# Another hand-written order for units 1 to 6 of phase one of a pooled-attention and snake-activation kernel

## The chip, the cores and the metric

The program runs on one NeuronCore of one Trainium2 chip. The metric is device microseconds of that core for one execution. Before the change three runs took 917.28, 917.67 and 918.19 us; the median, 917.67 us, is the time before.

## The reference

Attention of 8 batches with 8 heads, 576 rows and 64 columns, whose keys and values are means over 8 rows (72 pooled rows are left); its output, 4608 tokens by 512, goes through a layer of 2048 with the activation h + sin(alpha h)^2 / alpha:

```python
k_p = k.reshape(B, H, Sp, pool, D).mean(axis=3)
v_p = v.reshape(B, H, Sp, pool, D).mean(axis=3)
scores = scale * np.matmul(q, k_p.transpose(0, 1, 3, 2))
scores = scores - np.max(scores, axis=-1, keepdims=True)
attn = np.exp(scores)
attn = attn / (np.sum(attn, axis=-1, keepdims=True) + 1e-09)
x = np.matmul(attn, v_p)          # then to (4608, 512)
h = x @ w_in
s = np.sin(alpha * h)
out = (h + s * s / (alpha + 1e-09)) @ w_out
```

All arrays are float32.

## The kernel before, in words

**Two phases.** Phase one computes the attention and g = h + sin^2 / alpha and stores g to a buffer in HBM (`g_bridge`); phase two (from about 520 us) loads g and multiplies by w_out. Both large products are written with seven block products in place of eight (names M1 to M7); in phase one the products 1 and 5 of most groups are split once more in the same way ("inner products", steps i.a to i.e).

**Units and groups.** Phase one runs over 9 units of 512 columns of x (u = 0 to 8), each of 4 groups J = 0 to 3. A group multiplies a quarter of w_in: `M2`, `M6`, `M3`, `M7`, `M4` (line 930), each in four pieces (`M2.0` to `M2.3`), and M5 as well in group 1. Inner products (line 1020) of group J of units 2 to 6, and of groups 1 to 3 of unit 1, have the steps a, b, d, e1 and e5 on TensorE, with copies ca, cm, cb on ScalarE (lines 1033, 1037, 1040) and one sum ad on VectorE (line 1043) between them: b waits for ca, d for cb, e1 and e5 for ad. ScalarE copies partial sums from one PSUM bank to another (c16, c67, p5; line 911) and computes sines and squares (s00, s01, s10, s11, q00, q01, q1; lines 998 and 1005); VectorE adds them up (a00, a01, a11, f10, f1; line 910). f1 alone of these adds two SBUF operands (128 x 1024); the others read one operand from PSUM. `st` stores a group's g, 1 MB in two DMAs (line 1053); its tile is one of two, so a00 of the group after next waits for the store.

**The attention beside it.** While unit u (1 to 6) runs, the attention of batch u + 1 is done in its gaps: scores0 and scores1 (line 405), the shifts by the maximum (shift0 to shift3 name four calls that take the next of a list, so a swap of two names alone changes nothing; lines 425, 426), the exponentials (line 451), the sums and scalings norm0 to norm3 (VectorE lines 457, 458, GpSimd line 459), 32 x 32 transposes turn0 to turn3 on VectorE (lines 591 to 601) into the tile `tr`, sixteen DMAs `move` from `tr` to another partition quarter each (line 611), the products with v (`values`, lines 700, 713) and the copies out0 to out4 of the result (line 627). Beside it the operands of the batches behind are made ready: `load_q` (lines 185, 206) for unit u + 2, its transposes qa, qb, qc into `tr` (lines 318, 321) and sixteen DMAs back from `tr`, eight in qd and eight in qe (line 331); load_k0 and load_k1 (line 222) and load_v (lines 241, 246), and their sums over 8 rows on GpSimd: pool_k0, pool_k1, pool_vm (line 232, the large tile of v) and pool_v (lines 232, 252, the small rest). scores0 reads what qd wrote, scores1 what qe wrote too. k_t and k_c turn the pooled keys (lines 363, 367). load_k0, load_k1 and load_v take turns on two buffers named `kvin`; load_k1 waits until the first of the two that is pooled, in program order, is read.

**What sets the order.** Nothing is scheduled by the compiler: each engine and each DMA queue works through its instructions in program order, and that order comes from a list of actions with a number each. The tables `ORDER` (lines 42 to 138) give the numbers: "U" for the attention's actions in units 1 to 6, "mid0" to "mid3" for the four groups of units 1 to 6 (two groups are exceptions: the first of unit 1 uses "enter", the last of unit 6 "exit", neither of which changes). An action of table "U" stands at 28 u plus its number, one of a group at 7 (4 u + J) plus its number; `perform` sorts and emits them:

```python
for m, f in acts.items():
    if m in where:
        self.at(7 * n + where[m], f)
...
self.agenda.sort(key=lambda x: x[:2])
while self.agenda and self.agenda[0][0] < until:
    self.agenda.pop(0)[2]()
```

Waits between engines follow from the data, whatever the numbers. All DMAs of phase one's units 1 to 6 are issued by SyncE (SP), one queue; a DMA also waits until the one issued eight before it has landed.

Of the kernel before, what the change touches and what calls it, by code (L numbers as in the profile page):

```python
# [67 lines left out]
    "a00": 2.6351, "a11": 2.7835, "M3.1": 3.71335, "M3.2": 3.97525, "M3.3": 5.35825, "M4.0": 5.57345, "a01": 5.76695, "M4.1": 6.46705, "M4.2": 9.07915,  # L68
    "M4.3": 9.1098, "s11": 9.29485, "s10": 9.36555, "q1": 9.36695, "s01": 9.43775, "q01": 9.4416, "f1": 9.6118, "f10": 9.61195, "st": 10.05},
"end3": {  # L70
    "M5.0": -5.29345, "M5.1": -4.88305, "M1.0": -2.98805, "M1.1": -2.4027, "M1.2": -2.23625, "M5.2": -1.2153, "M1.3": -1.07205, "c16": 2.27975,
    "M6.0": 2.32495, "M6.1": 2.33055, "M6.2": 2.3529, "M2.0": 2.3654, "M6.3": 2.3726, "c67": 2.37425, "M2.1": 2.38685, "M2.2": 2.4012, "M5.3": 2.40185,
    "M7.0": 2.41595, "M2.3": 2.4234, "M7.1": 2.4277, "M7.2": 2.46025, "p5": 2.48725, "M3.0": 2.53015, "M7.3": 2.5939, "a11": 2.612, "M3.1": 2.6266,
    "s00": 2.7151, "q00": 2.82195, "s11": 2.9428, "M3.2": 2.96575, "M3.3": 2.96605, "a01": 3.3439, "M4.0": 3.50965, "a00": 3.60325, "M4.1": 3.9026,
    "M4.2": 4.2433, "M4.3": 4.37135, "s01": 4.63625, "q01": 4.6412, "s10": 4.64555, "q1": 6.5869, "f1": 6.6127, "f10": 6.6139, "st": 10.05},
"enter": {
    "M1.0": -0.48095, "M1.1": -0.4801, "M1.2": -0.4681, "M5.0": -0.45225, "M5.1": -0.44225, "M1.3": -0.4418, "M5.2": 0.0977, "M5.3": 0.1635, "c16": 0.2794,
    "p5": 0.86945, "M6.0": 2.04465, "M2.0": 3.2741, "M6.1": 6.62085, "M6.2": 6.6329, "M6.3": 6.6653, "M2.1": 6.6889, "M2.2": 6.8691, "M2.3": 7.1328,
    "c67": 7.13695, "s00": 7.13705, "q00": 7.13865, "a00": 9.0381, "M7.0": 10.78275, "M7.1": 10.8224, "M3.0": 10.85505, "M3.1": 10.97425, "M7.2": 11.40445,
    "M3.2": 11.41515, "M3.3": 11.59405, "M7.3": 11.633, "a01": 11.64185, "a11": 11.7721, "s01": 11.88975, "M4.0": 11.9007, "M4.1": 11.96155,  # L80
    "M4.2": 12.03945, "M4.3": 12.084, "q01": 12.2488, "s11": 12.2491, "s10": 12.51005, "q1": 13.17745, "f10": 13.40255, "f1": 13.6228, "st": 15.95645},
# [1493 lines left out]
```

## Time and profile before

| what | value |
|---|---|
| three runs, us | 917.28, 917.67, 918.19 |
| span of the profiled execution, first to last instruction, us | 915.5 |
| mean granted TensorE clock | 1.000 |
| TensorE busy, whole span | 98% |
| VectorE, ScalarE, GpSimd busy, whole span | 74%, 50%, 23% |
| units 2 to 5: start of the first scores, us | 147.7, 204.8, 262.1, 318.6 |
| start of the first scores of unit 6, us | 376.4 |
| mean busy share of the 16 DMA engines, 92 to 440 us | 0.63 |

The spans of one execution are shorter than its time by what lies around them; the profile does not say which of the three times belongs to the profiled execution. In the profile a matmul in float32 is two rows (two passes); rows of the timeline merge equal instructions that follow each other, with the start, the length, and in brackets the idle time of the engine before it and what ended it. In a row of waits the numbers are the total in us, how often, and the longest. In a row of windows they are the length and the busy us (with the number of instructions) of PE, its weight loads, VectorE (DVE), ScalarE (ACT) and GpSimd (POOL), then the granted clock, the DMA share and GB/s.

### The profile page before, as it was taken

The page shows a single profiled execution, that of the slowest core. Times are in us where ns is not written, and L with a number is a line of the kernel's source. Part 1 is how long each engine was busy: PE and PEld are TensorE (multiplying, and loading weights), DVE is VectorE, ACT ScalarE, POOL GpSimd, SP SyncE. Part 2 cuts the span into 40 slices and gives each one's busy share as a digit, 9 for nine tenths or more (in the row PEclk, how much of TensorE's full clock was granted, in tenths as well). Part 3 has the DMA queues.
Part 4 walks back from the last instruction along what each step waited for, and adds up shares of the span by engine and source line. Part 5 has one row for each costly group of instructions (what it writes and reads, how often), then busy time and mean ns, then how long its engine had stood idle before and what let it go on. Part 6 is the DMA issues. An engine that isn't in the chain of part 4 may idle for free.

```text
span 915.5 us, 18344 instructions
## 1 busy us (share of the span) xinstructions
PE 896.1 (98%) x7146; PEld 815.8 (89%) x7146; DVE 679.6 (74%) x1016; ACT 455.4 (50%) x1073; POOL 210.8 (23%) x235
## 2 busy tenths in 40 slices
PE   8999999999999999999999999999999999999998
PEld 5787888878788887888888899999999999999997
DVE  7576856768667585674466989978888888989895
ACT  5686877868778686787785722112111112112111
POOL 4689651733517334150000000000000000000000
PEclk9999999999999999999999999999999999999999
DMA  9946766666756766545627237171617253433501
GB/s 260 241 151 180 211 193 165 193 201 174 206 153 191 206 170 188 144 133 161 239 93 247 92 108 224 37 224 27 221 39 189 72 170 91 155 105 112 148 15 40
DMA packets 128751, 141.17 MB, mean 154 GB/s; under 512 B 46920, under 2 KB 95704, under 8 KB 128664
## 3 DMA queue, kind: packets, MB, share of 16 engines
q1 hardware_dynamic: 125880, 137.88, 51.6%
q10 hardware_dynamic: 2784, 2.11, 0.9%
q8 instruction: 57, 0.93, 0.4%
q14 instruction: 30, 0.25, 0.1%
HBM read 75.37 MB, written 47.19 MB: 134 GB/s over the span
## 4 chain that ended last, share of the span: by engine, by line
PE 79%; SPq 5%; DVE 4%; DMA 4%; ACT 3%; POOL 2%; issue 2%; ACTq 0%; DVEq 0%; POOLq 0%
PE PS L1306 42%; PE PS L930 28%; SPq L331 3%; DVE h L910 3%; PE PS L1020 3%; DMA kvin<-in_k_dram 2%; PE PS L700 2%; SPq L611 2%; DMA q<-tr 1%; POOL kvin L232 1%; PE PS L405 1%; ACT s L998 1%; ACT s L1005 1%; PE PS L713 1%; DMA ex<-tr 1%
## 5 line engine op out<-in xcount | busy, mean ns | idle before, releaser
L930 PE MATMUL PS<-home,a 128*128 128x256 f32 x968 | 250.1, 382 | 0.0
L930 PEld LDWEIGHTS PS<-home,a 128*128 128x128 f32 x968 | 177.9, 190 | 29.2 <-issue 5.0
L930 PE MATMUL PS<-home,as 128*128 128x256 f32 x728 | 194.6, 382 | 0.1
L930 PEld LDWEIGHTS PS<-home,as 128*128 128x128 f32 x728 | 132.7, 190 | 17.5 <-ACT PS L911 1.7
L1306 PE MATMUL PS<-s,wb 128*128 128x144 f32 x896 | 119.2, 286 | 0.4 <-ACT PS L1434 0.4
L1306 PEld LDWEIGHTS PS<-s,wb 128*128 128x128 f32 x896 | 113.6, 190 | 0.6 <-ACT PS L1434 0.6
L1356 POOL TENSOR_TENSOR cc<-cc,cb 128x576 f32<-128x576 f32 x1 | 2.0, 1981 | 484.6 <-DVE cb L1261 484.6
L1005 ACT ACTIVATE s<-s,c 128x256 f32<-128x256 f32 (+1 forms) x216 | 112.5, 580 | 0.0
L910 DVE TENSOR_TENSOR h<-PS,s 128x512 f32<-128x512 f32 x72 | 48.2, 683 | 74.8 <-ACT s L1005 72.9
L1434 ACT COPY PS<-PS 128x144 f32<-128x144 f32 x56 | 14.7, 263 | 144.4 <-PE PS L1306 144.3
L232 POOL TENSOR_TENSOR kvin<-kvin 96x768 f32<-96x768 f32 (+3 forms) x42 | 71.6, 1705 | 23.9 <-DMA kvin<-in_k_dram 15.8
L1306 PE MATMUL PS<-r,wb 128*128 128x144 f32 x512 | 73.2, 286 | 0.0
L1306 PE MATMUL PS<-s,a 128*128 128x144 f32 x512 | 73.2, 286 | 0.0
L910 DVE TENSOR_TENSOR h<-h,s 128x1024 f32<-128x1024 f32 x36 | 49.2, 1366 | 30.4 <-ACT s L1005 30.3
L998 ACT ACTIVATE s<-h,al 128x256 f32<-128x256 f32 x144 | 63.5, 502 | 13.1 <-DVE h L910 13.0
L1306 PEld LDWEIGHTS PS<-r,wb 128*128 128x128 f32 x512 | 67.1, 190 | 0.1
L1306 PEld LDWEIGHTS PS<-s,a 128*128 128x128 f32 x512 | 67.0, 190 | 0.0
L998 ACT ACTIVATE s<-PS,al 128x256 f32<-128x256 f32 x144 | 60.5, 475 | 11.2 <-PE PS L930 8.8
L910 DVE TENSOR_TENSOR h<-PS,p 128x512 f32<-128x512 f32 x72 | 49.0, 685 | 18.5 <-PE PS L930 9.8
L911 ACT COPY PS<-PS 128x512 f32<-128x512 f32 x72 | 41.6, 578 | 40.3 <-PE PS L930 16.8
L459 POOL TENSOR_TENSOR ex<-ex,sm 128x576 f32<-128x576 f32 (+1 forms) x28 | 36.0, 1300 | 108.9 <-DVE sm L458 108.2
L1454 ACT COPY PS<-PS 128x144 f32<-128x144 f32 x56 | 14.7, 263 | 89.4 <-PE PS L1306 89.4
(217 smaller groups left out, 1536.1 us busy)
## 6 DMA issues: line engine op xcount, KB each, us to landing
g_bridge<-h SPq DMA_DIRECT2D x72, 512.0 KB
r<-g_bridge SPq DMA_DIRECT2D x31, 1152.0 KB
out_dram<-o SPq DMA_DIRECT2D x122, 72.0 KB
kvin<-in_k_dram SPq DMA_DIRECT2D x14, 576.0 KB
q<-in_q_dram SPq DMA_DIRECT2D x7, 1024.0 KB
kvin<-in_v_dram SPq DMA_DIRECT2D x14, 512.0 KB
ex<-tr SPq DMA_DIRECT2D x54, 92.0 KB
ex<-tr SPq DMA_DIRECT2D x54, 88.0 KB
```

What stands on the lines that cost most here:

```text
L232: self.nc.gpsimd.tensor_tensor(out=t[..., 0:w] if w > D else out, in0=t[..., 0:w], in1=t[..., w:2 * w], op=OP.add)
L331: nc.sync.dma_start(out=qm[32 * c:32 * c + 32, to:to + w], in_=tr[32 * a:32 * a + 32, k, at:at + w])
L459: nc.gpsimd.tensor_tensor(out=E(i), in0=E(i), in1=sm.unsqueeze(2).to_broadcast([P, n, Sp]), op=OP.mult)
L611: queue.dma_start(out=self.aT[r:r + 32, a, 0:w], in_=tr[32 * a:32 * a + 32, c, s, 0:w])
L700: nc.tensor.matmul(o[r:r + 64], w, x, start=start and i < 2, stop=False, skip_group_check=True)
L910: add = lambda o, x, y: nc.vector.tensor_tensor(out=o, in0=x, in1=y, op=OP.add)
L911: copy = lambda o, x: nc.scalar.copy(out=o, in_=x)
L930: nc.tensor.matmul(ps[:, jj, :], self.A[p][:, kk, f * P:(f + 1) * P], x[:, kk, :], start=(start and part == 0), stop=(kk == 1), skip_group ...
L998: self.nc.scalar.activation(out=G.s[:, i, jj, j, :], in_=src[:, jj], func=AF.Sin, scale=self.al[:, f:f + 1])
L1005: self.nc.scalar.activation(out=x, in_=x, func=AF.Square, scale=self.c[:, f:f + 1])
L1020: nc.tensor.matmul(out, W[m][:, G.J], self.X2[p][m], start=start, stop=True, skip_group_check=True)
L1306: nc.tensor.matmul(out, W[:, J // 2, J % 2, :], A[:, J, :], start=(start and J == 0), stop=(J == self.NJ - 1), skip_group_check=True)
```

## The change

Only numbers of the tables "U", "mid0", "mid1", "mid2" and "mid3" change; the other tables are wrapped differently and hold what they held. No instruction is added or removed. In the tables below each line is from the file; the lines of the other tables, that differ in their wrapping alone, are left out.

```diff
 "U": {
-    "load_k0": -3.31225, "load_v": -0.96965, "scores0": 3.279, "shift0": 5.5894, "shift1": 5.6395, "scores1": 7.66855, "shift2": 7.69635, "exp1": 10.5847,
-    "exp0": 11.4077, "exp2": 11.40805, "shift3": 11.6083, "exp3": 11.73155, "norm0": 11.785, "norm1": 11.8859, "norm3": 11.919, "norm2": 11.9294,
-    "pool_vm": 11.9323, "pool_v": 11.9332, "pool_k0": 12.01065, "turn1": 12.15105, "turn3": 12.264, "turn2": 12.2775, "load_q": 13.4176, "turn0": 15.964,
-    "load_k1": 17.85695, "move": 24.04575, "clean": 24.12855, "values": 24.12865, "qa": 24.1287, "out4": 24.12875, "pool_k1": 24.12885, "out0": 24.12885,
-    "qc": 24.12885, "qb": 24.12895, "mark": 24.12895, "out2": 24.129, "sx0": 24.1291, "inner_x": 24.12915, "out3": 24.33175, "k_t": 24.4364, "k_c": 24.4956,
-    "qd": 24.7856, "out1": 24.87145, "sx1": 24.87995, "sx2": 25.5786, "qe": 26.19775, "sx3": 33.60825},
+    "load_k0": -3.31225, "load_v": -0.96965, "scores0": 3.279, "shift1": 5.61994, "shift0": 7.14828, "scores1": 7.66855, "shift2": 7.69635,
+    "exp1": 11.39419, "exp0": 11.40678, "shift3": 11.6083, "exp2": 11.69571, "exp3": 11.73155, "norm0": 11.85811, "norm2": 11.9294, "norm1": 11.93006,
+    "norm3": 11.93036, "pool_k0": 11.93266, "pool_v": 11.93269, "pool_vm": 11.9327, "turn2": 12.31331, "turn3": 12.32741, "turn1": 12.34345,
+    "load_q": 13.4176, "load_k1": 13.54022, "turn0": 15.964, "move": 24.04575, "clean": 24.12855, "values": 24.12865, "qc": 24.12868, "qa": 24.1287,
+    "out4": 24.12875, "pool_k1": 24.12885, "out0": 24.12885, "qb": 24.12895, "mark": 24.12895, "out2": 24.129, "sx0": 24.1291, "inner_x": 24.12915,
+    "out3": 24.33175, "k_t": 24.4364, "k_c": 24.4956, "qd": 24.64897, "out1": 24.87145, "sx1": 24.87995, "qe": 24.96216, "sx2": 25.5786,
+    "sx3": 33.62096},
...
 "mid0": {
-    "i.a": -3.44775, "i.ca": -3.11535, "i.cm": -3.1115, "i.b": -3.11065, "i.cb": -3.1106, "i.d": -2.748, "i.ad": -1.9601, "i.e5": -0.69805, "p5": 2.55425,
-    "i.e1": 2.87235, "c16": 3.3461, "M2.0": 3.50525, "M2.1": 4.52555, "M6.0": 5.9571, "M2.2": 5.9617, "M2.3": 5.96715, "M6.1": 6.2838, "M6.2": 7.6624,
-    "M6.3": 7.66535, "s00": 7.835, "q00": 8.92395, "c67": 9.6177, "a00": 10.37115, "M3.0": 11.33615, "M3.1": 11.33625, "M7.0": 11.34, "M3.2": 11.34015,
-    "M7.1": 11.4021, "M3.3": 11.41255, "a01": 11.6089, "M7.2": 11.68785, "M7.3": 11.70765, "s01": 11.7474, "a11": 11.8728, "M4.0": 11.9812, "M4.1": 12.0337,
-    "M4.2": 12.03755, "M4.3": 12.0423, "s11": 12.2488, "s10": 12.24975, "q1": 12.4368, "q01": 12.8354, "f10": 12.95975, "f1": 12.96, "st": 13.86795},
+    "i.a": -3.44775, "i.ca": -3.11535, "i.cm": -3.1115, "i.b": -3.11065, "i.cb": -3.1106, "i.d": -2.748, "i.ad": -1.9601, "i.e5": -0.69805,
+    "p5": 2.55425, "i.e1": 2.87235, "c16": 2.92563, "M2.3": 4.30308, "M6.1": 5.96453, "M2.2": 5.96455, "M2.0": 5.96456, "M6.2": 6.04054,
+    "M2.1": 6.30017, "M6.0": 6.77211, "M6.3": 7.50001, "s00": 7.835, "c67": 8.14526, "M3.2": 8.48782, "q00": 8.92395, "M7.0": 9.2981, "a00": 10.37115,
+    "M3.0": 11.33615, "M7.1": 11.4021, "M3.1": 11.40333, "M3.3": 11.41255, "a01": 11.6089, "M7.3": 11.68745, "M7.2": 11.68785, "s01": 11.7474,
+    "a11": 11.86757, "s11": 11.89308, "M4.2": 11.92875, "M4.1": 11.94559, "M4.0": 11.9812, "M4.3": 12.0423, "s10": 12.24975, "q01": 12.2689,
+    "q1": 12.30265, "f1": 12.96, "f10": 13.64418, "st": 13.86795},
 "mid1": {
-    "i.a": 4.34025, "i.ca": 4.3997, "M5.0": 4.40225, "i.b": 4.4051, "i.cb": 4.4067, "i.cm": 4.4072, "M5.1": 4.415, "i.d": 4.41525, "i.ad": 4.61795,
-    "M5.2": 4.68665, "i.e1": 4.6893, "c16": 4.6958, "M6.0": 4.70895, "M2.0": 4.71385, "M6.1": 4.71905, "M6.2": 4.85125, "M6.3": 4.88645, "M2.1": 4.9164,
-    "M2.2": 4.9175, "M2.3": 4.9216, "M5.3": 4.9236, "c67": 4.9407, "s00": 4.9412, "M3.0": 5.0296, "M7.0": 5.0386, "M7.1": 5.0393, "M3.1": 5.10295,
-    "q00": 5.1499, "a00": 5.2457, "p5": 5.24655, "M7.2": 5.26125, "M7.3": 5.26325, "a11": 5.3567, "M3.2": 5.4866, "M3.3": 5.9075, "M4.0": 5.9184,
-    "a01": 5.95985, "M4.1": 5.9935, "M4.2": 6.1266, "M4.3": 7.29135, "s10": 7.7045, "s01": 7.82565, "s11": 7.82645, "q1": 7.8273, "f10": 9.63095,
-    "q01": 10.3848, "f1": 10.57355, "st": 17.5694},
+    "i.a": 4.34025, "i.ca": 4.3997, "i.b": 4.4051, "i.cm": 4.40677, "i.cb": 4.40681, "M5.0": 4.41522, "i.d": 4.41525, "i.ad": 4.61795,
+    "M5.2": 4.68665, "i.e1": 4.6893, "c16": 4.6958, "M6.0": 4.70895, "M2.0": 4.71385, "M6.1": 4.71905, "M6.2": 4.85125, "M6.3": 4.90912,
+    "M2.1": 4.9164, "M2.2": 4.9175, "M2.3": 4.9216, "M5.1": 4.92644, "M5.3": 4.93039, "c67": 4.9407, "s00": 4.9412, "M3.0": 5.00874, "M7.0": 5.04209,
+    "M7.1": 5.04209, "M3.1": 5.10295, "q00": 5.1499, "p5": 5.21406, "a00": 5.2457, "M7.3": 5.25744, "M7.2": 5.26125, "a11": 5.3567, "M3.3": 5.9075,
+    "M3.2": 5.9142, "M4.0": 5.9184, "a01": 5.95985, "M4.2": 5.96632, "M4.3": 5.96725, "M4.1": 5.9935, "s01": 7.82565, "s10": 7.91743, "s11": 7.9648,
+    "q1": 8.02211, "f10": 9.63095, "q01": 10.3848, "f1": 10.57355, "st": 17.5694},
 "mid2": {
-    "i.a": -2.3038, "i.cm": -1.7518, "i.ca": -1.7514, "i.b": -1.7503, "i.cb": -1.7501, "i.d": -1.735, "i.ad": -1.59855, "i.e1": -1.0348, "c16": -0.57955,
-    "M6.0": 0.29225, "M2.0": 0.293, "i.e5": 0.29845, "M6.1": 0.33965, "M6.2": 0.3757, "M6.3": 0.39735, "M2.1": 0.41675, "M2.2": 0.4244, "M2.3": 0.5874,
-    "c67": 1.0048, "s00": 1.0277, "q00": 1.0698, "p5": 1.70115, "a00": 1.96485, "M7.0": 2.16015, "M7.1": 2.53405, "M3.0": 2.6511, "M7.2": 2.70895,
-    "M7.3": 2.7296, "M3.1": 2.8176, "M3.2": 2.9094, "M3.3": 3.08845, "a11": 3.2776, "a01": 3.78395, "s11": 3.99815, "M4.0": 4.0048, "s01": 4.0872,
-    "M4.1": 4.23675, "M4.2": 4.25385, "M4.3": 4.44025, "s10": 9.67355, "q1": 9.71865, "f10": 10.1286, "q01": 10.88815, "f1": 11.0343, "st": 11.5035},
+    "i.a": -2.3038, "i.cm": -1.7748, "i.ca": -1.7514, "i.b": -1.7503, "i.cb": -1.7501, "i.d": -1.735, "i.ad": -1.59855, "i.e1": -1.0348,
+    "c16": -0.57955, "M6.1": -0.42395, "M6.0": -0.01556, "M6.3": 0.37336, "M2.1": 0.37512, "M6.2": 0.3757, "M2.0": 0.39898, "M2.2": 0.47325,
+    "M2.3": 0.59072, "i.e5": 0.69826, "c67": 1.0048, "s00": 1.0277, "q00": 1.21555, "a00": 1.96485, "M3.2": 2.08265, "p5": 2.22096, "M7.0": 2.57527,
+    "M3.0": 2.6511, "M7.2": 2.70895, "M7.3": 2.7296, "M7.1": 2.7919, "M3.1": 2.8176, "M3.3": 3.08845, "a11": 3.2776, "M4.0": 3.73108, "a01": 3.78395,
+    "s11": 3.99815, "s01": 4.0872, "M4.1": 4.10256, "M4.2": 4.26342, "M4.3": 4.44025, "s10": 9.71301, "q1": 9.71865, "f10": 10.1286, "q01": 10.88815,
+    "f1": 11.0343, "st": 11.5035},
 "mid3": {
-    "i.a": -6.2122, "i.cm": -5.4897, "i.ca": -4.6089, "i.b": -4.1596, "i.cb": -3.09295, "i.d": -3.08935, "i.ad": -3.08745, "i.e1": -2.73575, "c16": 1.9205,
-    "i.e5": 2.24095, "p5": 2.8146, "M6.0": 2.95315, "M6.1": 2.99055, "M2.0": 3.0069, "M6.2": 3.03045, "M6.3": 3.0506, "M2.1": 3.07885, "c67": 3.10355,
-    "M2.2": 3.17395, "M7.0": 3.2504, "M2.3": 3.37095, "M3.0": 3.3757, "M3.1": 3.552, "M7.1": 3.5522, "s00": 3.61515, "M7.2": 3.6319, "M7.3": 3.6631,
-    "q00": 3.85525, "a00": 3.8687, "a11": 3.8995, "M3.2": 4.0691, "M4.0": 4.2482, "M3.3": 4.2522, "a01": 5.04005, "M4.1": 5.62885, "M4.2": 6.2931,
-    "M4.3": 9.7245, "s10": 10.13465, "s11": 13.67425, "q1": 13.86355, "s01": 14.5847, "q01": 18.3923, "f1": 18.6301, "f10": 18.85055, "st": 19.1827},
+    "i.a": -5.44769, "i.cm": -5.07042, "i.ca": -4.6089, "i.b": -4.1596, "i.cb": -3.09295, "i.d": -3.08935, "i.ad": -3.08745, "i.e1": -2.73575,
+    "c16": 1.9205, "i.e5": 2.24095, "p5": 2.8146, "M6.2": 3.03045, "M6.0": 3.03297, "M2.0": 3.03902, "M6.3": 3.0506, "M6.1": 3.06611, "M2.1": 3.07812,
+    "c67": 3.12872, "M2.3": 3.19906, "M2.2": 3.37148, "M7.1": 3.37179, "M3.2": 3.40969, "M7.0": 3.55213, "M3.1": 3.55217, "M7.3": 3.60051,
+    "s00": 3.61515, "M7.2": 3.6319, "M3.0": 3.77507, "q00": 3.85525, "a00": 3.8687, "a11": 3.8995, "M4.0": 3.95088, "M3.3": 3.96749, "a01": 5.04005,
+    "M4.2": 5.27798, "M4.1": 6.29603, "s11": 10.02061, "M4.3": 10.06132, "s10": 10.13465, "s01": 11.30312, "q1": 13.86355, "q01": 18.61556,
+    "f1": 18.6301, "f10": 18.80556, "st": 19.1827},
```

What that makes of the order on the engines in a unit (from the two built programs, unit 3):

- SP before: load_k0 of the next unit, qd, store of group 2, qe, load_v; after: qd, load_k0, qe, store of group 2, load_v. And before: store of group 0, load_k1, the moves; after: load_k1, store of group 0, the moves.
- GpSimd before: norm0, norm1, norm3, norm2, pool_vm, pool_v, pool_k0; after: norm0, norm2, norm1, norm3, pool_k0, pool_v, pool_vm. Then, as before, clean (a memset) and pool_k1.
- VectorE: norm and turn in other orders (turns 2, 3, 1 for 1, 3, 2; a00 of group 1 ahead of them); f10 of group 0 behind f1 and ahead of turn0; a11 of group 0 ahead of the second norm; f10 of the unit before ahead of norm0; qc ahead of qa.
- ScalarE: c16 of group 0 ahead of the sines s10, s11 of the unit before; s11 of group 0 ahead of c67 of group 1; the order of q01 and q1, of s01 and s10 of groups 0 and 1, of c67 and the square beside it, and of two exponentials and the copies cb and cm beside them; the small copy within `values` (line 707) ahead of c67 of group 3.
- TensorE: products of one group or of two neighbours exchanged. Between i.d and i.e1 of group 3 stand M4.1 and M4.2 where M4.0, M4.1 and M4.2 stood; in group 1, M5.1 stands behind M2.3 and no longer ahead of i.d; i.e5 of group 2 stands behind M2.3 where it stood behind M2.0.

55 rows, old and new, of the table ORDER are left out of this document.

## The prediction

> **What bounds the kernel now.** I read the busy shares first, then the busy time unit by unit in phase one (a unit is four groups on 512 columns; its scores start at 147.7, 204.8, 262.1, 318.6 and 376.4 us), then what TensorE (PE) waited for there, then the timeline around each wait.
>
> ```profile
> PE 896.1 (98%) x7146; PEld 815.8 (89%) x7146; DVE 679.6 (74%) x1016; ACT 455.4 (50%) x1073; POOL 210.8 (23%) x235
> 204.80:262.10 57.30, 55.30 (x471) 47.05 (x470) 39.57 (x64) 42.91 (x97) 24.32 (x28) 1.00 0.65 185
> 318.60:376.40 57.80, 55.19 (x470) 47.53 (x469) 37.96 (x64) 42.76 (x97) 23.69 (x28) 1.00 0.60 172
> PE PS L405 <- DMA q<-tr: 4.0, 5, 1.1
> PE PS L700 <- DMA ex<-tr: 3.8, 3, 1.8
> PE PS L1020 <- DVE PS L1043: 1.9, 2, 1.0
> ```
>
> PE is busy 98%, at a granted clock of 1.00. A unit needs 55.1 to 55.3 us of PE and takes 56.5 to 57.8: order can win only the difference. From 92 to 440 us three waits make up nearly all of it: 4.0 us in the second scores (q's last piece, units 2 to 6: 1.12, 0.87, 0.63, 0.79, 0.56), 3.8 in the values (softmax moves, units 1, 4, 5: 1.26, 0.72, 1.81), 1.9 in the inner products of group 3 (units 2, 3). Sum 9.7; nothing the change touches can give more.
>
> ```profile
> 201.81 0.89 SPq L1053 DMA_DIRECT2D g_bridge<-h  x2
> 202.75 7.03 SPq L331 DMA_DIRECT2D q<-tr  x8
> 211.36 1.00 PE L405 MATMUL PS<-kblk,q 64*64 64x72 f32 x46 [0.87 <-DMA q<-tr]
> 346.34 0.90 SPq L1053 DMA_DIRECT2D g_bridge<-h  x2
> 347.33 0.82 SPq L222 DMA_DIRECT2D kvin<-in_k_dram  x1
> 348.25 12.88 SPq L611 DMA_DIRECT2D ex<-tr  x16
> 362.79 0.65 PE L700 MATMUL PS<-ex,vm 64*64 64x512 f32 x6 [1.81 <-DMA ex<-tr]
> 225.79 3.73 POOL L232 TENSOR_TENSOR kvin<-kvin 128x1024 f32<-128x1024 f32 x2
> 231.37 1.26 DVE L910 TENSOR_TENSOR h<-h,s 128x1024 f32<-128x1024 f32 x1
> 240.47 3.74 POOL L232 TENSOR_TENSOR kvin<-kvin 96x768 f32<-96x768 f32 x2 [2.95 <-DMA kvin<-in_k_dram]
> 240.53 2.83 DVE L910 TENSOR_TENSOR h<-h,s 128x1024 f32<-128x1024 f32 x1
> ```
>
> The reader sees three late things. The last eight q copies (qe) stand behind the store of group 2, which waits for its last addition until 201.8, so they end at 209.8 and land at 211.2. The sixteen moves stand behind the second k load: its 576 KB go first, and issue stops for it. And f1 takes 2.83 us where its median is 1.23, because a k addition on GpSimd (POOL) began 0.06 us before it.
>
> **q copies first (qd, qe).** The sixteen q copies now stand ahead of the next unit's first k load (qd) and of group 2's store (qe). In unit 3 qd ended at 256.3; then the k load (0.82) and eight copies of about 0.64 (move rows: 11.37 for sixteen, less a 0.8 pause) end near 262.4 and land 1.5 later, 264; the second half of the scores wants them near 267.5. Cover 3.5 us: the whole 4.0 us goes. Late next is the store: issued near 262.5 instead of 259.1, it lands 4.5 later, 267, and its buffer is wanted by the next unit's a00 at 269.4: 2.4 us of cover, cost nothing; uncovered it would delay a00, then a01 and the inner sum, at most by what is missing. The k load, 9 us later, is first read after the next softmax (282 in unit 4). The v load behind the store starts earlier than before.
>
> **k pooled and loaded ahead of the moves.** POOL now does k's sums (3.56) first, then the small v sums (2.5), then the large ones (4.5). The second k load needs a free buffer; that comes from k's sums at about 229.4 in unit 3, not from the large v sums at 230.3, and its place is now ahead of group 0's store (232.66), which it leaves alone. The moves then stand right behind that store and the last turn (233.44) instead of starting at 234.57 with a pause of 0.8 (in unit 5, 1.5 to 2.7 lost). They end some 1.9 us earlier, 3 in unit 5. Units 1, 4, 5 lacked 1.26, 0.72 and 1.81, but PE also arrives earlier by the q wait (0.6 to 0.9): just enough in unit 5. I take 3.2 of 3.8; in unit 1 the margin below is thin. Bounds 1.5 and 3.8. The large v sums end near 237; their reader starts at 248.8.
>
> **f1 of group 1 and the inner sum behind it.** With k landed near 234, the second k pooling follows at about 237 and ends near 241, so f1 (240.5, or a little before) meets its tail, not its head: some 0.3 lost, not 1.6. But the order also takes a product pair away between inner step d and step e1 of group 3 (two of 0.432 us, there were three). DVE's chain behind ACT's copy ca is 0.9 (q01) + 1.22 (f1) + 0.6 + 0.7 = 3.4, plus hand-over 0.1; PE's way from ca is 0.1 + 0.88 + 0.86 + 0.45 + 0.86 = 3.15. So a wait of up to 0.35, less where PE reaches step b late: 0.2 in each of six units, 1.2 new (bounds 0 and 2.1), against 1.9 removed.
>
> **Products, copies and turns exchanged.** Work is neither added nor removed. I followed unit 3 product by product. c16 of group 0 moves ahead of the sine s10; a00 of group 1 ahead of the turns (224.9 to about 224.4), which lets ca of group 2 keep up with its inner products, now 0.43 earlier; f10 of group 0 goes behind f1, so f1 is 0.69 earlier and the turn where it was. M5.1 moves out of the stretch before c16 of group 1, leaving that copy about 0.05 of cover where it had 0.56. In group 2 ACT runs from c16's end (232.41) to ca's end (239.68) in 7.27 while PE needs 7.87 to step b: 0.6 of cover. Five such places have under 0.15 left; I price them at 0.15 a unit, 0.9 (bounds 0 and 3.0, half a microsecond a unit).
>
> **Sum.** 4.0 + 3.2 + 1.9 - 1.2 - 0.9 = 7.0 less. The profiled span is 915.5; the runs are 917.28 to 918.19, so some 2.2 lie around it. 915.5 - 7.0 + 2.2 = 910.7. Its own range: best 4.0 + 3.8 + 1.9 = 9.7, giving 908.0; worst 4.0 + 1.5 + 1.9 - 2.1 - 3.0 = 2.3, giving 915.4.
>
> **Rivals.** A, slower: f1 of group 0 is caught by the large v sums. Their first step takes 2.37 us, and now starts behind k's and the small v sums, 0.05 + 3.56 + 2.5 = 6.1 after the last softmax product on POOL. f1 started 5.54 after it in units 2 to 5 (225.83 to 231.37) and 6.45 in unit 1; without f10 ahead it is 4.85 and 5.76. So 1.25 and 0.34 of margin; the rival decides as soon as f1 comes later than 6.1. Behind f1 wait the turn, the store and the next group's sines; of 2.37 ACT's cover takes 0.3, so 2.1 in each of units 1 to 5, 10.5 in all: 910.7 + 10.5 = 921.2. For it: 2.83 above; at 125.96 an f1 that began 0.02 before a k step took 1.22. Against it: the margin, and that PE, from which f1 follows, comes earlier. The Trainium skill, "SBUF — State Buffer", section "Who interferes with whom", states it as a lock: a vector operation with two SBUF inputs and a GpSimd operation that reads SBUF exclude each other, and whichever is issued first holds the ports to its end. By that rule the additions with one PSUM input are safe; the trace agrees (92 of them between 92 and 440 us, none over 0.69 us).
>
> B: the moves stay late, because the store's 1 MB now stands directly ahead of them as k did, and the exchanged products cost their bound: 4.0 + 1.0 - 2.1 = 2.9, giving 914.8. For it: moves share the queue with the store in every unit. Against: in unit 3 the store had landed at 237.1, before the moves were eight deep.
>
> C: nothing is gained, since ACT's chain takes over from the copies that land: if f1 and the sines behind it hold ca back by 1.2 us in each of six units, 7.2 more, 917.9. For it: the small covers. Against: ACT is busy 43 of 57 us in a unit and waits for PE more than PE for it.
>
> **How the numbers follow.** Forecast 0.67, A 0.12, B 0.12, C 0.09. A measurement of this kernel can tell 0.2%, 1.8 us, from no change: faster means under 915.8. Faster 0.67 + 0.12 = 0.79, same 0.09, slower 0.12. The range starts at 907.5, just under the best case, and ends at 917.0, so A and most of C lie outside.
>
> **What would show it.** After: no wait of the second scores (L405) for q copies; the values (L700) wait for moves in no unit, or in unit 1 alone; the k load (L222) issued before the store of group 0; f1 (L910, h from h and s) under 1.6 us everywhere; a short new wait of L1020 for the inner sum (L1043). Wrong it would be if f1 of group 0 shows 2 us and more, if waits of L930 or L1020 for ACT add up to over 3 us, or if a00 waits for a store.

## The result and the profile after

Four runs of the changed kernel took 907.51, 907.82, 909.42 and 911.21 us, median 908.62. Four runs of the kernel before on the same chip took 917.28 to 918.33, median 917.93. The ratio is 0.9898, with a 95% interval of 0.988 to 0.9915: about 1% faster. The forecast was 910.7, its range 907.5 to 917.0. The profiled execution took 907.51 us and spans 905.7 us (before: 915.5).

All line numbers of the changed kernel are higher by 9: L405 is now L414, L700 is L709, L910 is L919, L911 is L920, L930 is L939, L1020 is L1029, L1033 is L1042, L1043 is L1052.

First the busy shares of the changed kernel:

```profile
PE 896.0 (99%) x7146; PEld 815.0 (90%) x7146; DVE 677.4 (75%) x1016; ACT 456.6 (50%) x1073; POOL 206.3 (23%) x235
```

TensorE (PE) is busy for the same 896 us as before, in a shorter span: the gain is idle time of PE. All that the rows show of PE's waits between 92 and 440 us (total, times, longest):

```profile
PE PS L1029 <- ACT PS L1042: 0.9, 1, 0.9
PE PS L939 <- ACT PS L920: 0.6, 1, 0.6
```

All three rows of before that the prediction names (4.0 for q, 3.8 for the moves, 1.9 for the inner sum) are gone, and so is a fourth (0.4 for ScalarE, in unit 1). In their place stand 1.5 us of waits for ScalarE, both in unit 1. The busy time unit by unit, changed kernel, units 1 to 4 (length, then busy us of PE, weight loads, DVE, ACT, POOL):

```profile
91.22:147.71 56.49, 54.88 (x466) 46.63 (x465) 40.14 (x64) 41.37 (x93) 28.53 (x38) 1.00 0.67 191
147.71:202.66 54.95, 54.95 (x470) 47.00 (x469) 37.99 (x64) 43.02 (x97) 23.52 (x28) 1.00 0.67 192
202.66:257.40 54.74, 54.74 (x471) 46.88 (x470) 38.02 (x64) 43.03 (x97) 23.53 (x28) 1.00 0.69 194
257.40:312.09 54.69, 54.69 (x470) 46.98 (x470) 38.02 (x64) 43.03 (x97) 23.54 (x28) 1.00 0.67 192
```

From unit 2 on the length of a unit is the recorded busy time of PE, to the hundredth; unit 1 alone keeps 1.6 us of idle time. Busy time is not yet a floor, though. In these traces a product of 128x256 is recorded with 0.38 us, while the next one starts 0.22 after it when nothing holds it up, so a hold-up of up to 0.16 us hides in the product ahead of it, and a longer one hides as much. That is why a unit's busy time is smaller than the 55.1 to 55.3 of before: it held a part of the waits that are gone. The scores of unit 3, for instance, were busy for 3.07 us before and for 2.78 after, with the q wait gone.

The q copies, the store and the second half of the scores in unit 3; then the k load, the store, the moves and the values in unit 5 (SyncE's queue and PE, changed kernel):

```profile
196.63 5.52 SPq L340 DMA_DIRECT2D q<-tr  x8
202.25 1.07 SPq L1062 DMA_DIRECT2D g_bridge<-h  x2
207.48 1.53 PE L414 MATMUL PS<-kblk,q 64*64 64x72 f32 x80
...
334.87 0.33 SPq L231 DMA_DIRECT2D kvin<-in_k_dram  x1
338.26 0.98 SPq L1062 DMA_DIRECT2D g_bridge<-h  x2
339.67 11.51 SPq L620 DMA_DIRECT2D ex<-tr  x16
353.47 0.65 PE L709 MATMUL PS<-ex,vm 64*64 64x512 f32 x6
```

The copies end at 202.15, 0.5 us before unit 3's first scores; before they ended 4.9 us after them. The scores at 207.48 wait for no copy. The moves of unit 5 start 27.6 us after the unit's first scores (29.6 before), end at 351.2, which is 3.4 us earlier in the unit (the forecast said 3), and the values at 353.47 come without a wait.

For the rest I use one sum per profile, worked out from the start times of matmul rows: the **stretch**, from unit 1's first scores to phase two's first product. It leaves out the start, where loads arrive: unit 1's first scores came between 90.6 and 94.3 us in the profiles of this study. It took 433.45 us before and 423.70 after, 9.75 less; the span fell by 9.8.

### The profile page after: what moved, and what is told of

Read it like the earlier page. It is cut to its first block, busy times and chain, and to the rows that moved or that the text cites. A ratio compares the mean times of both kernels' runs of the same rounds, so it can differ in the third digit from the quotient of the medians.

```text
span 905.7 us, 18360 instructions
## 1 busy us (share of the span) xinstructions
PE 896.0 (99%) x7146; PEld 815.0 (90%) x7146; DVE 677.4 (75%) x1016; ACT 456.6 (50%) x1073; POOL 206.3 (23%) x235
## 4 chain that ended last, share of the span: by engine, by line
PE 95%; ACT 2%; DVE 2%; issue 0%; DMA 0%; ACTq 0%; DVEq 0%
PE PS L1315 42%; PE PS L939 39%; PE PS L1029 7%; PE PS L414 2%; PE PS L709 2%; DVE h L919 1%; PE PS L722 1%; ACT s L1007 1%; ACT s L1014 1%; PE PS L1087 0%; PE PS L523 0%; PE PS L502 0%; PE PS L372 0%; PE PS L485 0%; DMA out_dram<-o 0%
## 5 line engine op out<-in xcount | busy, mean ns | idle before, releaser
L939 PE MATMUL PS<-home,a 128*128 128x256 f32 x968 | 252.2, 382 | 0.0
L939 PEld LDWEIGHTS PS<-home,a 128*128 128x128 f32 x968 | 177.5, 190 | 28.9 <-issue 5.0
L939 PE MATMUL PS<-home,as 128*128 128x256 f32 x728 | 196.8, 381 | 0.6 <-ACT PS L920 0.6
L939 PEld LDWEIGHTS PS<-home,as 128*128 128x128 f32 x728 | 133.9, 190 | 17.7 <-ACT PS L920 1.0
L919 DVE TENSOR_TENSOR h<-PS,s 128x512 f32<-128x512 f32 x72 | 48.5, 686 | 81.7 <-ACT s L1014 81.7
L919 DVE TENSOR_TENSOR h<-h,s 128x1024 f32<-128x1024 f32 x36 | 48.2, 1340 | 29.8 <-ACT s L1014 29.8
L920 ACT COPY PS<-PS 128x512 f32<-128x512 f32 x72 | 41.4, 575 | 40.4 <-PE PS L939 16.1
L1315 PE MATMUL PS<-s,we 128*128 128x144 f32 x384 | 55.0, 286 | 0.7 <-ACT PS L1418 0.7
```

What stands on the lines that cost most here:

```text
L919: add = lambda o, x, y: nc.vector.tensor_tensor(out=o, in0=x, in1=y, op=OP.add)
L920: copy = lambda o, x: nc.scalar.copy(out=o, in_=x)
L939: nc.tensor.matmul(ps[:, jj, :], self.A[p][:, kk, f * P:(f + 1) * P], x[:, kk, :], start=(start and part == 0), stop=(kk == 1), skip_group ...
L1315: nc.tensor.matmul(out, W[:, J // 2, J % 2, :], A[:, J, :], start=(start and J == 0), stop=(J == self.NJ - 1), skip_group_check=True)
```

## The experiments

Each kernel was timed beside the kernel before on the same chip, and the chips differ, so ratios are compared, not microseconds alone. The stretch and the units are those of one profiled execution each.

| kernel | median us (runs) | ratio to before, 95% | stretch, us | units 1 to 5, us |
|---|---|---|---|---|
| before | 917.93 (4) | 1 | 433.45 | 56.06, 57.16, 57.26, 56.51, 57.82 |
| after | 908.62 (4) | 0.9898 (0.988 to 0.9915) | 423.70 | 56.49, 54.95, 54.74, 54.69, 54.88 |
| q_only | 912.92 (5) | 0.9912 (0.9892 to 0.9931) | 428.37 | 56.32, 55.68, 55.92, 56.29, 56.38 |
| k_only | 914.95 (5) | 0.9932 (0.9912 to 0.9951) | 431.23 | 56.82, 58.48, 55.67, 56.20, 55.43 |
| qk | 908.37 (4) | 0.9864 (0.9842 to 0.9886) | 423.47 | 56.44, 54.63, 54.80, 55.04, 54.78 |
| mid_only | 917.82 (11) | 0.9969 (0.9954 to 0.9985) | 435.41 | 55.41, 60.15, 56.11, 57.73, 57.10 |
| q_back | 913.16 (8) | 0.9946 (0.9926 to 0.9966) | 428.04 | 56.54, 57.01, 55.53, 55.53, 55.48 |
| guard | 905.75 (4) | 0.9866 (0.9849 to 0.9883) | 421.99 | 54.29, 55.02, 54.87, 54.83, 55.02 |
| vm_first | 905.35 (4) | 0.9858 (0.9843 to 0.9872) | 421.92 | 54.71, 54.89, 54.73, 54.70, 54.89 |
| qk_vm | 906.47 (4) | 0.9866 (0.983 to 0.9902) | 423.11 | 56.00, 54.71, 54.81, 54.67, 55.14 |
| collide | 906.96 (4) | 0.9866 (0.9839 to 0.9892) | 422.40 | 54.61, 54.89, 54.74, 54.70, 54.88 |
| after_third | 908.29 (4) | 0.9878 (0.985 to 0.9906) | 423.84 | 56.69, 54.88, 54.74, 54.70, 54.88 |
| caught | 911.79 (5) | 0.9919 (0.9893 to 0.9944) | 427.67 | 55.86, 55.99, 55.76, 55.73, 56.38 |

### The parts alone: q_only, k_only, qk, mid_only

Four numbers of the table "U" for k, two for q (the entries stand apart in the table); `qk` has both, all on the kernel before. `mid_only` has the new group tables with the old table "U".

```diff
 # q_only
-    "qd": 24.7856, "qe": 26.19775,
+    "qd": 24.64897, "qe": 24.96216,
 # k_only
-    "pool_vm": 11.9323, "pool_v": 11.9332, "pool_k0": 12.01065, "load_k1": 17.85695,
+    "pool_k0": 11.93266, "pool_v": 11.93269, "pool_vm": 11.9327, "load_k1": 13.54022,
```

> The kernel before with qd and qe alone moved (qd ahead of the next unit's first k load, qe ahead of the store of group 2). Theory (three separate late things, each worth its own wait): no wait of the second scores for q copies, 4.0 us less in that row; but PE then reaches the values up to 0.9 us earlier per unit with the moves where they were, so 1 to 2 us come back as waits of the values (L700) for moves: 914.5 to 916. Rival (the waits add up independently): 4.0 less in all, 913.9. Rival (ACT's chain takes over): no change, 917.9.

> The kernel before with pool_k0, pool_v, pool_vm in this order and load_k1 ahead of the store of group 0, nothing else. Theory: the values wait for moves in no unit (3.8 us less), f1 of group 1 is 1.3 us in units 2 and 3 (1.9 less of waits L1020 for L1043); q's wait of 4.0 stays. But f10 still stands ahead of f1 of group 0, so f1 starts 5.5 us after the last softmax product on POOL in units 2 to 5 and 6.4 in unit 1, against 6.1 for the first large v sum: unit 1 collides (f1 over 3 us), units 2 to 5 just miss. 912.5 to 914.5. Rival A (the collision in all units): f1 of group 0 over 3 us in five units and the time at 918 or more.

> Both of these together in the kernel before, all products, copies, turns and softmax steps as they were. Theory: the two parts carry the whole gain and the exchanges none: 908 to 910.5, as the changed kernel, and waits for q copies and for moves both gone. Rival (the exchanges are needed, because the chains of ACT and VectorE bind once PE is not held by DMA): 912 or more, with waits of L930 and L1020 for ACT and DVE that the changed kernel does not have.

> The four tables of the groups from the changed kernel with the attention's table of the kernel before. Theory: the order of products alone removes no DMA wait; q's 4.0 and the moves' 3.8 stay, the inner sum's 1.9 stays: 916.5 to 919. Rival (the exchanges of products are what gains): 913 or less.

What PE waited for from 92 to 440 us, q_only:

```profile
PE PS L700 <- DMA ex<-tr: 5.0, 4, 1.5
PE PS L1020 <- DVE PS L1043: 0.9, 1, 0.9
PE PS L1020 <- ACT PS L1033: 0.5, 1, 0.5
```

the same of k_only:

```profile
PE PS L405 <- DMA q<-tr: 4.3, 5, 2.0
PE PS L700 <- DMA ex<-tr: 0.9, 1, 0.9
PE PS L930 <- ACT PS L911: 0.6, 1, 0.6
PE PS L1020 <- ACT PS L1033: 0.3, 1, 0.3
```

of qk:

```profile
PE PS L700 <- ACT PS L911: 0.5, 1, 0.5
PE PS L930 <- ACT PS L911: 0.5, 1, 0.5
PE PS L1020 <- ACT PS L1033: 0.5, 1, 0.5
```

and of mid_only (its lines are 8 higher than those of before):

```profile
PE PS L708 <- DMA ex<-tr: 4.6, 5, 1.8
PE PS L413 <- DMA q<-tr: 4.3, 5, 2.0
PE PS L1028 <- DVE PS L1051: 0.3, 1, 0.3
```

Each part takes away its own wait (all of q's, 2.9 of 3.8 for the moves), and what is left of the other grows: without the q wait PE comes earlier at the values and waits 5.0 us for the moves where it waited 3.8; with the moves earlier it waits 4.3 for q where it waited 4.0, with a longest of 2.0 in place of 1.1. The stretch falls by 5.1 us with q alone, 2.2 with k alone, 10.0 with both.

That looks as if the two parts together were worth 2.7 us more than the two added, but two of these profiles hold something else. The granted clock was 0.50 for 3.4 us of unit 2 in k_only (first row) and in mid_only (second row):

```profile
154.99:158.40 3.41, 3.25 (x50) 2.87 (x51) 1.90 (x3) 1.18 (x3) 0.00 (x0) 0.50 0.90 190
156.26:159.66 3.40, 3.40 (x12) 2.87 (x11) 1.61 (x2) 0.54 (x2) 0.00 (x0) 0.50 1.02 202
```

Four products of 128x256 took 1.89 us there (k_only, at 156.81), where they take 1.03 otherwise. No other profile of the table has such a piece. Half of 3.4 is 1.7 us, an estimate of what it cost at most; it is in the 58.48 and 60.15 us of unit 2. So k alone is worth between 2.2 and 3.9, and the two together 1.0 to 2.7 more than the parts added. The times show no such thing: 0.88% less for q alone and 0.68% for k alone make 1.56%, and both together took 1.36% less (1.14 to 1.58). Whether the parts help each other stays open; that each makes the other's wait longer is shown.

`qk` holds all of the changed kernel's gain (423.47 against 423.70). In k_only and qk f1 of group 0 was caught in unit 1, as it is in the changed kernel (2.86 and 2.72 us; see below). The exchanges of products, copies and turns alone take most of the inner-sum wait away (0.3 left of 1.9), and the DMA waits take as much back (8.9 us against 7.8). The stretch of mid_only is 2.0 us longer than before, up to 1.7 of it (the estimate above) from the clock; its eleven runs took 0.15 to 0.46% less time than before. What the exchanges alone are worth stays open within that. On top of the two DMA parts they add nothing that these profiles show.

Of the expectations, that of qk held, and that of q_only held for the waits (1.2 us came back at the values), while its time fell more than either sum said. k_only came out above its range (914.95), with 0.9 us of the moves wait left in unit 1. mid_only lost the inner-sum wait that I had expected to stay.

### One part taken back: q_back

```diff
-    "qd": 24.64897, "qe": 24.96216,
+    "qd": 24.7856, "qe": 26.19775,
```

> The changed kernel with qd and qe back at their old places. Theory: the waits of the second scores for q copies return with 0.6 to 1.1 us a unit, and some more because the rest now runs ahead: 4 to 6 us, 912.5 to 915. Rival (the gain of the q part was only room for the rest): no more than 2 us.

PE's waits from 92 to 440 us in q_back:

```profile
PE PS L414 <- DMA q<-tr: 3.1, 4, 1.8
PE PS L1029 <- ACT PS L1042: 0.9, 1, 0.9
PE PS L939 <- ACT PS L920: 0.6, 1, 0.6
```

The q wait is back (3.1 us) and the stretch 4.3 longer than after, as expected, while unit 1's two waits for ScalarE stand as they did: they have nothing to do with q.

### Unit 1 of the changed kernel, and f1 of group 0

Rival A spoke of f1 of group 0, caught by the large v sums. It happened, in unit 1. VectorE, the first two large sums on GpSimd, ScalarE and PE there, changed kernel (start, length, and in brackets the idle time before):

```profile
116.16 3.35 DVE L919 TENSOR_TENSOR h<-h,s 128x1024 f32<-128x1024 f32 x1
116.08 4.57 POOL L241 TENSOR_TENSOR kvin<-kvin 128x1024 f32<-128x1024 f32 x2
119.55 0.91 ACT L1007 ACTIVATE s<-h,al 128x256 f32<-128x256 f32 x2 [3.15 <-DVE h L919]
122.51 0.70 PE L939 MATMUL PS<-home,as 128*128 128x256 f32 x2 [0.62 <-ACT PS L920]
126.68 0.49 PE L1029 MATMUL PS<-last,q 128*128 128x128 f32 x2 [0.88 <-ACT PS L1042]
```

The first large step began 0.08 us before f1, which took 3.35 us in place of 1.2. ScalarE stood idle for 3.15 us until f1's result came, and its late copies held PE up twice, 6 and 10 us on. Unit 2 of the same profile has the opposite order:

```profile
172.55 1.30 DVE L919 TENSOR_TENSOR h<-h,s 128x1024 f32<-128x1024 f32 x1
172.16 0.61 POOL L261 TENSOR_TENSOR vz<-vr,mask 128x256 f32<-128x256 f32 x1
172.73 3.35 POOL L241 TENSOR_TENSOR kvin<-kvin 128x1024 f32<-128x1024 f32 x1
```

Here f1 began 0.18 us ahead of the step, took 1.30, and the step took 3.35 in place of 2.37. The Trainium skill, "SBUF — State Buffer", section "Who interferes with whom", says that the second to issue is blocked until the first is through. The trace agrees, in both directions: 3.35 for f1 in unit 1, 3.35 for the step in unit 2.

Two kernels take this order away. `guard` puts a 128x1 addition on GpSimd, which reads f1's result and so waits for it, ahead of the large sums (six more instructions). `vm_first` adds nothing: it puts the large sums ahead of the small ones.

```diff
 # guard
+    def late_vm(self, u):
+        x = self.groups[4 * u].g[:, 0, 0, 1, 0:1]
+        self.nc.gpsimd.tensor_tensor(out=self.sm.tile([P, 1], F32, name="seen")[:], in0=x, in1=x, op=OP.add)
+        self.pool_vm()
-    "pool_v": 11.93269, "pool_vm": 11.9327
+    "pool_v": 11.93269, "pool_vm": 13.63
 # vm_first
-    "pool_v": 11.93269, "pool_vm": 11.9327
+    "pool_vm": 11.93268, "pool_v": 11.9327
```

> The changed kernel with one addition of 128 x 1 on GpSimd ahead of the large v sums that reads f1's result of group 0, so that these sums cannot start before f1 has ended. Theory (the rest of PE's waits, 1.5 us in unit 1, and the spread of the changed kernel's four runs, 907.5, 907.8, 909.4, 911.2, both come from f1 of group 0 meeting the first large v sum): f1 of group 0 is 1.3 us in every unit, PE's two waits in unit 1 are gone, and all runs lie within 1 us near 906.0 to 906.6. Rival (the spread has another cause): the runs spread over 3 us as before, whatever f1 does. Rival (POOL, now idle until f1's end, is late with the v sums or the second k pooling): waits of the values for pooling, 908 or more.

> The changed kernel with the large v sums ahead of the small ones, so that their first step (2.37 us) begins 3.6 us after the last softmax product and f1 of group 0 falls into it in units 1 to 5. Theory (lock; whichever starts first holds it): f1 of group 0 takes 1.9 to 2.7 us in units 1 to 5, PE waits for ACT at step b of group 2, 0.5 to 1.5 us a unit: 910 to 914. Rival (f1's time does not reach PE): f1 long, but the time within 1 us of the changed kernel. Rival (no lock): f1 at 1.3 us.

Both take unit 1 from 56.5 to 54.3 and 54.7 us, the list of PE's waits between 92 and 440 us is empty in both, and both come to 905.4 to 905.8 us; four runs of vm_first lie between 904.96 and 905.45. My expectation of vm_first was wrong: I had f1 caught in every unit. VectorE and GpSimd of vm_first in units 1 and 2:

```profile
115.55 1.22 DVE L919 TENSOR_TENSOR h<-h,s 128x1024 f32<-128x1024 f32 x1
113.14 2.38 POOL L241 TENSOR_TENSOR kvin<-kvin 128x1024 f32<-128x1024 f32 x1
...
170.11 1.32 DVE L919 TENSOR_TENSOR h<-h,s 128x1024 f32<-128x1024 f32 x1
167.99 2.36 POOL L241 TENSOR_TENSOR kvin<-kvin 128x1024 f32<-128x1024 f32 x1
```

f1 now comes as the first large step ends (at 115.52) or in its last 0.24 us (170.35), so 0.1 us is all that it loses. What matters is not whether the two meet but how much of the step is left when f1 is issued. vm_first has the lowest median and the shortest stretch of all versions here; its ratio and guard's are not told apart by their intervals.

### What a caught f1 costs: collide and caught

`collide`, written from guard, was to bring unit 1's case about in every unit: the same small addition, but reading an earlier result (a11 of group 1), so that the sums would start about 1 us ahead of f1 (six more instructions).

```diff
-        x = self.groups[4 * u].g[:, 0, 0, 1, 0:1]
+        x = self.groups[4 * u + 1].g[:, 1, 0, 1, 0:1]
-    "pool_vm": 13.63
+    "pool_vm": 12.6
```

> The changed kernel with a 128x1 addition on GpSimd that reads the first result of group 1 (a11), put ahead of the large v sums, so that their first step begins about 1 us ahead of f1 of group 0 in every unit: what the changed kernel meets in unit 1 alone, made to happen everywhere. Theory (f1 of group 0 waits for the end of the step, and TensorE's next product waits for it): f1 of group 0 takes 2.3 to 3.4 us in units 1 to 5, TensorE waits 0.7 to 1.6 us for ScalarE in each, 426 to 430 us from unit 1's first scores to phase two's first product, 909 to 913 in all. Rival (the longer f1 is hidden behind ScalarE's and TensorE's other work outside unit 1): f1 as long, waits of TensorE under 0.3 us in units 2 to 5, 422 to 424.5 us from unit 1's first scores, 905.5 to 908.5 in all.

It missed. The small sums ahead of it end only 0.24 us after f1 starts, so the new addition stood behind f1 itself, and f1 took 1.21 to 1.33 in units 1 to 5. It does free unit 1 (54.61 us), a third time, and catches f1 of unit 6 (2.51 us). `caught` then moves one GpSimd operation of 0.61 us, the multiplication that ends the small sums, behind the large ones:

```diff
-        def pool():
+        def pool(z=True):
             self.pool_rows(x, x[:, 0:D])
+            if z:
+                pool_z()
+
+        def pool_z():
             nc.gpsimd.tensor_tensor(out=vz[:], in0=x[:, 0:D].unsqueeze(1).to_broadcast([P, H // 2, D]),
...
-"pool_v": lambda: self.pool_v(), "pool_vm": lambda: self.pool_vm()
+"pool_v": lambda: self.pool_v(False), "pool_vm": lambda: (self.pool_vm(), self.pool_z())
```

> The changed kernel with one GpSimd operation moved: the multiplication that ends the small v sums (128x256, 0.61 us) goes behind the large v sums, so that the first large step begins some 0.4 us ahead of f1 of group 0 in units 2 to 5 instead of 0.18 behind it. No work is added. Theory (f1 of group 0 waits for the step's end and TensorE waits for what follows from it, as in unit 1 of the changed kernel): f1 of group 0 takes 2.9 to 3.4 us in units 2 to 5, TensorE waits 1.2 to 1.7 us for ScalarE in each, each of these units is 1.4 to 2.2 us longer (56.1 to 57.1), 429.5 to 433 us from unit 1's first scores to phase two's first product, 913.5 to 918 in all. Rival (outside unit 1 the longer f1 is covered by ScalarE's and TensorE's other work): f1 as long, units 2 to 5 under 55.4 us, 423 to 426 us from unit 1's first scores, 907 to 911 in all.

VectorE, GpSimd, ScalarE and PE in unit 2 of caught (its lines are 4 higher than those of the changed kernel):

```profile
173.30 2.94 DVE L923 TENSOR_TENSOR h<-h,s 128x1024 f32<-128x1024 f32 x1
172.81 4.57 POOL L241 TENSOR_TENSOR kvin<-kvin 128x1024 f32<-128x1024 f32 x2
176.28 0.91 ACT L1011 ACTIVATE s<-h,al 128x256 f32<-128x256 f32 x2 [2.10 <-DVE h L923]
183.41 0.49 PE L1033 MATMUL PS<-last,q 128*128 128x128 f32 x2 [0.77 <-ACT PS L1046]
```

and its PE's waits for ScalarE from 92 to 440 us:

```profile
PE PS L1033 <- ACT PS L1046: 3.9, 5, 0.9
```

f1 loses 1.7 us in each of units 2 to 5 (2.93 or 2.94 against 1.22), as expected, and PE waits for it once a unit, 10 us later, at step b of group 2, where ScalarE's copy ca is late. The row of that wait shows 0.76 to 0.77 of the 1.7, and units 2 to 4 are 1.0 us longer (unit 5, where the values also wait 0.2 for moves, 1.5), not 1.4 to 2.2; 911.79 us lies between my two expectations. So ScalarE's chain from f1 to that copy has about 0.7 us of cover there: 1.7 less 1.0.

### Do the exchanges matter once f1 is free: qk_vm

`qk` with the large sums first:

```diff
-    "pool_vm": 11.9323, "pool_v": 11.9332
+    "pool_vm": 11.93268, "pool_v": 11.9327
```

> The kernel before with the two DMA-order parts alone (q copies ahead; k pooled and loaded ahead of the moves) and, within the pooling, the large v sums ahead of the small ones. Nothing of the exchanges of turns, moves and group products. Theory (the exchanges are worth nothing once f1 of unit 1 no longer meets a large v sum): within 1.5 us of the version with all of the change and the large sums first, 904.5 to 907 us; from unit 1's first scores to phase two's first product 421.5 to 423 us. Rival (the exchanges keep f1 off GpSimd's sums, which the older order does not): f1 of group 1 or of group 0 takes over 2.3 us in two units or more, TensorE waits for ScalarE 1.5 us or more in all, 424 to 426 us from unit 1's first scores, 907.5 to 910 in all.

906.47 us against vm_first's 905.35 on another chip, with ratios of 0.9866 and 0.9858 that the intervals don't tell apart. In the stretch qk_vm is 1.2 us longer, nearly all of it in unit 1 (56.00 against 54.71), where its values wait 1.0 us for the moves:

```profile
PE PS L700 <- DMA ex<-tr: 1.0, 1, 1.0
PE PS L1020 <- ACT PS L1033: 0.5, 1, 0.5
PE PS L700 <- ACT PS L911: 0.2, 1, 0.2
```

So by these two profiles the exchanges are worth some 1 us, in the one unit where the moves are still tight; f1 stayed at or under 1.77 in all units, so the rival's reason isn't found.

### The changed kernel again

The changed kernel was run twice more: beside guard and vm_first, and beside qk_vm and collide.

> The changed kernel once more, for its spread and one more profile. Theory: times fall into steps near 907.5, 909.4 and 911.2, by the number of units of 2 to 5 in which f1 of group 0 starts after the first large v sum (0.18 us of margin in the profile there is); this profile shows as many f1 of over 2.5 us in these units as its time is steps of 1.7 to 1.9 above 907.5. Rival: times spread evenly, with f1 near 1.3 us in units 2 to 5 in every profile.

> The changed kernel once more, for a second profile of it. Theory (what differs between executions is the start, ahead of unit 1's first scores, where loads arrive): from unit 1's first scores to phase two's first product 423.2 to 424.2 us as in the first profile (423.7), f1 of group 0 in units 2 to 5 again under 1.4 us, while unit 1's first scores may begin anywhere from 90.5 to 94.5 us. Rival (f1's margin of 0.18 us ahead of the first large v sum is lost in some executions): f1 of group 0 over 2 us in one of units 2 to 5 and that unit 1.0 to 2.0 us longer than the others.

The first of the two took 907.57, 907.94 and 908.03 us; a fourth execution took 3303.27 us, and the one profile is of that, so it shows nothing of f1. The profile of the second repeats that of the first section: stretch 423.84 (423.70), unit 1 56.69 (56.49), f1 of group 0 1.30 to 1.33 in units 2 to 5, 3.33 in unit 1. The spread of the runs is not settled by it. In all, the other eleven runs took 907.27 to 908.03 (seven), 909.12 to 909.42 (three) and 911.21 (one), and both profiles are of runs at 907.5. Such gaps would fit one or two more units in which f1 loses its 0.18 us of lead (unit 1 costs some 2), and vm_first's four runs lie within 0.5 us; but guard, whose sums can't begin before f1 is through, spreads by 2.4. It is not the granted clock: the four longer runs list a mean of 0.999 or 1.000, as the seven do, where the run profiled for k_only, with its 3.4 us at half clock, lists 0.998. No profile shows one of the four.

## Why the prediction was right, point by point

**The size.** 7.0 us were forecast and 9.8 are gone from the span. From unit 1 to phase two PE's idle time fell by 8.6 and its recorded matmul time by 1.1; the start came 0.4 earlier, and phase two has 0.4 more idle time. (Around the span lie 1.8 us, where I had taken 2.2.) 8.6 is also what the rows of waits give: 10.1 gone (9.7, and the 0.4 for ScalarE) and 1.5 new.

**q copies first: right in place and size.** All 4.0 us of waits went, and the store behind the copies made nobody wait. Alone, the part is worth 5.1 us of stretch; taken back it costs 4.3. That it is more than the row of the wait fits the part that hides in the busy time, 0.3 us in the scores of a unit (3.07 for 2.78). My bound of 9.7 ("nothing the change touches can give more") missed that: I took 55.1 to 55.3 us as what a unit needs, and after the change it took 54.69 to 54.95.

**k ahead of the moves: right, a little small.** 3.2 of 3.8 was forecast, and all 3.8 went, unit 1's part too. The sum allowed for PE's earlier arrival. On top of q the part is worth 4.9 us of stretch (428.37 to 423.47); alone 2.2 to 3.9, as said above.

**f1 of group 1 and the inner sum.** The removed 1.9 went; f1 of group 1 takes 1.28 to 1.30 in units 2 to 5 and meets the tail of the k sums, as forecast. The 1.2 of new waits came too, though no row of PE's waits shows it. It stands at the weight loads (units 2 to 5, changed kernel), and in the start times of the products (unit 3):

```profile
PEld PS L1029 <- DVE PS L1052: 3.1, 8, 0.4
238.44 0.38 PE L1029 MATMUL PS<-last,q 128*128 128x128 f32 x2
238.66 0.39 PE L1029 MATMUL PS<-ex,aM 128*128 128x128 f32 x2
238.88 1.03 PE L939 MATMUL PS<-home,a 128*128 128x256 f32 x4
239.89 0.49 PE L1029 MATMUL PS<-home,aM 128*128 128x128 f32 x2
240.21 0.39 PE L1029 MATMUL PS<-ex,a 128*128 128x128 f32 x2
```

The row of four products takes 1.03 us, 0.38 of it the last one, so they start 0.216 apart, and the next one could start at 239.74; the one that needs the inner sum starts at 239.89, and it and its fellow take 0.32 us to the next row (239.89 to 240.21), where such a pair takes 0.22 (238.44 to 238.66). So 0.25 us are lost, all of it inside lengths that count as busy. In group 3 that happens once in each of units 1 to 6: 1.5 us against the 1.2 forecast, at the place and by the chain that the forecast names. The second such wait of a unit stands in group 0 of the next one, where products came 0.09 to 0.18 late before as well, so little of it is new.

**Products, copies and turns exchanged.** 0.9 was priced, and the rows show nothing in units 2 to 5; what stays under 0.16 us a place they could not show. It also did not gain: qk has all of the stretch's 9.8 without the exchanges.

**Rival A came true in unit 1 alone.** Place and mechanism were right, both numbers were not. The margin of 1.25 us in units 2 to 5 was 0.18: in unit 2 the sums ahead of the large ones take 5.83 us from their start, right behind the last softmax product (6.1 forecast), and f1 comes 5.65 after that start, where I had 4.85, the old distance less f10. I moved f1 by the operation taken from in front of it (0.69) against a softmax that stays. But in unit 3, counted from the first scores, the sums behind the softmax now start 1.75 us earlier (19.20 for 20.95) and f1 1.69 earlier (24.84 for 26.53): the q wait that is gone (0.87 in its row) moves both, and the softmax gained as much again. In unit 1 the margin of 0.34 came out at -0.08. The price was mis-sized the other way: 2.1 a unit, where a hold of 1.7 costs 1.0 to 1.5 (caught) and the 2.1 of unit 1 some 2 (56.5 and 56.7 against 54.3 to 54.7), since the cover in units 2 to 4 is about 0.7 and not 0.3. Caught in all of units 1 to 5, the changed kernel would have been some 4 us slower (caught: 427.67 of stretch against 423.70), still faster than before. The 92 additions with one PSUM input that the prediction counts are those from 120 to 440 us; from 92 on there are 100, and none takes over 0.69 either. Rivals B and C are out: no moves are waited for, and ScalarE's chain takes over nowhere but in unit 1.

The errors had opposite signs. In the rows: 7.0, with 0.9 and 0.6 priced too dear, 0.4 not thought of and the 1.2 that no row shows, less 1.5 of new waits in unit 1, which the sum held at nothing: 8.6. In the busy time: 1.5 lost to the inner sum and yet 1.1 less in all, so some 2.6 (by difference) went with the waits that are gone, and that was not in the sum. The mechanism was right in its two main terms; that the total came as near as 2.8 us is in part luck, since these errors cancel.

## What to carry to other kernels

Two waits that follow each other in a loop are judged together: taking one away brings the engine earlier to the other, whose row grew here from 3.8 to 5.0 us and from 4.0 to 4.3. Before comparing two profiles, look at the granted clock piece by piece: 3.4 us at half clock made one part look up to 1.7 us worse than it is. When two engines share something that the first to come keeps to the end, an order with a lead of 0.2 us works only as long as nothing shifts; place the long operation so that the short one arrives at its end, which here cost one swap of two numbers and won 2.6 us more (907.94 to 905.35 on one chip). And an empty list of PE's waits doesn't mean that nothing is late: compare the start times of the products with their usual distance.

## What was not expected of the hardware

- Recorded matmul time holds a part of each wait: 55.13 to 55.26 us a unit before, 54.69 to 54.95 after (units 2 to 5), with the same matmuls at the same granted clock of 1.00, because the product ahead of a wait counts with its whole 0.38 us instead of 0.22. The Trainium skill, "Perfetto Trace Analysis", section "Identifying the Most-Contended Engine", calls matmul busy time a poor measure of how close a kernel is to its limit; these rows agree, and they put 0.2 to 0.5 us a unit to it.
- Between two GpSimd steps that follow at once, a waiting VectorE operation gets in: in unit 1 of the changed kernel f1 was issued 0.08 us behind the first step and was through at 119.51, while the two steps together took 4.57, to 120.65, where guard shows 3.71.
- A blocked operation shows no idle time in the profile: its own length grows (3.35, 2.94, 2.66 for f1, and 3.35 for a GpSimd step of 2.37), so it is found by comparing durations of one form, not in the rows of waits.
